# Attention output, z2 and z1 products with seven block products instead of eight, in one block of attention and gated MLP

## The chip, the cores and the metric

The kernel runs on one core of one Trainium2 chip. The metric is the device time of one execution in microseconds (us). Engines: PE is TensorE, DVE is VectorE, ACT is ScalarE, POOL is GpSimd, SP is the queue that issues most of the DMAs. PSUM is the memory into which PE writes its products, SBUF the one that holds the other tiles.

## The reference

One transformer block on 2048 tokens, model width D = 1024, bf16 in and out. Cut to what matters:

```python
h = layernorm(x) * (1 + ca) + sa
x = x + ga * (attention(h) @ wo)              # 32 heads of 128: [2048, 4096] @ [4096, 1024]
h = layernorm(x) * (1 + cb) + sb              # called h2 below
z = gelu(h @ w_in)                            # [2048, 1024] @ [1024, 3584]
z1 = z[..., :1792]
z2 = layernorm(z[..., 1792:])
g = w_sp @ z2 + b_sp[:, None]                 # [2048, 2048] @ [2048, 1792]: the "gate"
out = x + gb * ((z1 * g) @ w_out)
```

Four products come after attention: the attention output ("acc"), z2, z1, and the gate in two halves, each followed by half of the projection with `w_out`.

## The kernel before

Acc, z2 and z1 are plain products. One tile of 128 tokens is accumulated over all of the contraction in a PSUM bank, VectorE or ScalarE reads it once, and layer norm and modulation of the row follow in VectorE:

```python
# acc (L493 is the matmul), one tile of 128 tokens; cut
for n in cols:
    nc.tensor.matmul(accs[ti][n], lhs, wo_t[:, hh, sl], start=(hh == 0), stop=(hh == H - 1))
...
    nc.vector.tensor_mul(out=tmp[:], in0=accs[ti][n], in1=ga[:, sl])
    nc.vector.tensor_add(out=x1[:, sl], in0=tmp[:], in1=xts[ti][:, sl])
ln_mod(x1[:, :], mod2, hb)
nc.sync.dma_start(h2_dram[ti % 4], hb[:])          # and back with a transposing load

# z2 (L715), cut
for dc in range(KD):
    nc.tensor.matmul(zps[:], h2T[:, dc, ti * P:(ti + 1) * P], z2w[:, dc, sl],
                     start=(dc == 0), stop=(dc == KD - 1))
nc.scalar.activation(z2[:, sl], zps[:], ACT.Gelu_apprx_tanh)

# z1 (L793), cut: four banks of 512 tokens per 128 features
for dc in range(KD):
    nc.tensor.matmul(zps[:], w[:, dc, :], h2T[:, dc, q * 512:(q + 1) * 512],
                     start=(dc == 0), stop=(dc == KD - 1))
nc.scalar.activation(z1T[:, f, q * 512:(q + 1) * 512], zps[:], ACT.Gelu_apprx_tanh)
```

The gate is already computed with seven block products for eight (Winograd's form of Strassen's scheme). Operands are cut in 2 x 2 blocks; sums of blocks are formed once, seven products run, and the outputs are sums of products. The products accumulate in PSUM where they can, and VectorE saves a copy ("snap") where one partial sum serves two outputs:

```python
product(a, p, 1, True);  s = snap(p, 0)
product(c_, p, 2, True); emit(p, c_, s[:], 0, 0)               # output 11 = P1 + P2
product(a, p, 6, False); st[p]["x"] = snap(p, 0)               # P1 + P6
product(b_, p, 7, True)
product(a, p, 5, False); emit(p, b_, snap(p, 1)[:], 1, 1)      # output 22 = P1 + P6 + P5 + P7
product(a, p, 3, False); emit(p, a, b[1], 0, 1)                # output 12 = P1 + P6 + P5 + P3
product(b_, p, 4, False); emit(p, b_, x[:], 1, 0)              # output 21 = P1 + P6 + P7 + P4
```

The softmax here doesn't subtract the row's maximum and nothing guards it: scores larger than these inputs give would overflow.

## Time and profile before

| | before |
|---|---|
| time | 1838.55 us median of 4 runs (1837.13 to 1840.26) |
| PE busy | 1814.2 us, 99% of the profiled span of 1835.3 us |
| acc | 1151 to 1367 us, 0.216 us per matmul of 512 columns |
| z2 | 1367 to 1463.9 us: 512 matmuls of 448 columns, 96.9 / 512 = 0.189 us each |
| z1 | 1463.9 to 1560.6 us: 448 matmuls of 512 columns, 0.216 us each |

First the profile's page: busy time of each engine, and the busy tenths in 40 slices of the span, 45.9 us each. Acc, z2 and z1 lie in slices 26 to 34.

```profile
span 1835.3 us, 24790 instructions
...
PE 1814.2 (99%) x8926; PEld 834.8 (45%) x8926; DVE 1344.2 (73%) x2245; ACT 1135.4 (62%) x1199; POOL 32.5 (2%) x55
...
PE   7999999999999999999999999999999999999999
DVE  6998888888888988888888888544445502667664
ACT  6988999998998999999999999000003355003000
```

Read it by columns. PE is at 9 from the second slice to the last. DVE and ACT fall to 0 to 5 after attention: where the change works, only PE is full. So matmuls that are removed there should come straight off the time, as long as what replaces them fits into the other two engines.

The same by stage, from the windows of the trace (busy time of each engine inside each stretch): acc, z2, z1.

```profile
core 0: us, PE busy (x) PEld busy (x) DVE busy (x) ACT busy (x) POOL busy (x), PEclk, DMA share, GB/s
1161.00:1367.00 206.00, 206.00 (x956) 93.44 (x955) 92.73 (x166) 0.00 (x0) 8.23 (x15) 1.00 0.56 162
1367.00:1463.90 96.90, 96.90 (x514) 50.12 (x513) 59.73 (x119) 34.27 (x63) 8.77 (x16) 1.00 0.27 91
1463.90:1560.60 96.70, 96.70 (x450) 43.83 (x448) 14.82 (x24) 48.52 (x72) 0.55 (x1) 1.00 0.48 103
```

PE is busy for the whole of each stretch. The groups of instructions (last columns: busy us, mean ns of one | idle time of the engine just before them) give counts and say the same: no idle time before these matmuls.

```profile
L493 PE MATMUL acc<-wo_t,ot 128*128 128x512 bf16 x992 | 219.6, 379 | 0.0
...
L715 PE MATMUL zps<-z2w,h2T 128*128 128x448 bf16 x512 | 97.0, 352 | 0.0
L793 PE MATMUL zps<-h2T,z1w 128*128 128x512 bf16 x448 | 96.9, 379 | 0.0
```

The 379 ns is the length of one matmul's record; matmuls overlap, and what counts is the distance from one start to the next, 0.216 us for 512 columns and 0.189 us for 448.

Below, "lost" is the distance between the starts of consecutive matmuls less the pitch of the first, that is, the distance when nothing waits (columns / 2.4 + 2.6 ns, which gives the measured 0.216 and 0.189 us), summed over a stretch, without steps of one pitch where a record is missing. For the kernel before, acc, z2 and z1 lost 0.1 us, and gates and projections 5.5 us.

### The profile page before, as it was taken

Reading aid. Unit: us, or ns where it says so; the run is one execution under the profiler, and the core shown is the slowest. Engines: PE = TensorE matmul, PEld = TensorE weight load, DVE = VectorE, ACT = ScalarE, POOL = GpSimd, SP = SyncE. Lnnn points to the kernel's source line nnn. Section 1 sums busy time; section 2 is a strip of 40 time slices with the busy share of each in tenths; the row PEclk is TensorE's granted clock in tenths of the full one; section 3 lists DMA queues with packets and bytes.
Section 4 is the critical chain, followed back from the end, with each engine's and each line's share of the span. In section 5 each row is a group of like instructions: output and inputs, shape, how many; then the busy total and the mean of one; then the engine's idle time right before and its main releaser. Section 6 shows DMA issues by size and latency. Waiting matters only on the chain.

```text
span 1835.3 us, 24790 instructions
## 1 busy us (share of the span) xinstructions
PE 1814.2 (99%) x8926; PEld 834.8 (45%) x8926; DVE 1344.2 (73%) x2245; ACT 1135.4 (62%) x1199; POOL 32.5 (2%) x55
## 2 busy tenths in 40 slices
PE   7999999999999999999999999999999999999999
PEld 4444444444444444444444444444445544444444
DVE  6998888888888988888888888544445502667664
ACT  6988999998998999999999999000003355003000
POOL 1000000000000000000000000000000000000000
PEclk9999999999999999999999999999999999999999
DMA  7565465464564543555554434757423190436212
GB/s 241 139 160 127 127 162 135 135 167 121 138 163 131 163 125 93 144 164 129 149 154 135 123 108 114 225 164 204 119 64 110 73 214 1 148 94 188 75 52 75
DMA packets 431947, 245.70 MB, mean 134 GB/s; under 512 B 303440, under 2 KB 385616, under 8 KB 431824
## 3 DMA queue, kind: packets, MB, share of 16 engines
q1 hardware_dynamic: 431824, 244.13, 48.7%
q8 instruction: 69, 1.13, 0.3%
q14 instruction: 54, 0.44, 0.1%
HBM read 141.56 MB, written 52.97 MB: 106 GB/s over the span
## 4 chain that ended last, share of the span: by engine, by line
PE 93%; DMA 3%; DVE 2%; SPq 1%; issue 1%; ACT 0%; POOL 0%; DVEq 0%; POOLq 0%
PE sps L384 23%; PE ops L591 23%; PE acc L493 12%; PE qps L363 11%; PE zps L715 5%; PE bo L900 5%; PE zps L793 5%; PE a L818 4%; DMA zr<-z_dram 3%; PE b L818 2%; PE c L818 1%; DVE pacc L601 1%; DMA wm<-in_w_mod_dram 1%; PE mps L190 0%; DVE stats L143 0%
## 5 line engine op out<-in xcount | busy, mean ns | idle before, releaser
L579 ACT ACTIVATE pt<-sps 128x1024 bf16<-128x1024 f32 x1024 | 1018.9, 1024 | 105.0 <-PE sps L384 74.3
L601 DVE TENSOR_TENSOR pacc<-pacc,pt 128x1024 bf16<-128x1024 bf16 x896 | 616.4, 688 | 61.6 <-ACT pt L579 1.9
L591 PE MATMUL ops<-pt,v_sb 128*128 128x512 bf16 x2048 | 609.9, 379 | 1.2 <-DVE ou L597 1.2
L384 PE MATMUL sps<-qT,kT 128*128 128x512 bf16 x2048 | 608.9, 379 | 1.1 <-ACT pt L579 0.7
L363 PE MATMUL qps<-h1T,wq_t 128*128 128x512 bf16 x992 | 335.5, 379 | 0.5 <-DVE rec L452 0.4
L591 PEld LDWEIGHTS <-v_sb 128*128 128x128 bf16 x2048 | 200.1, 98 | 242.0 <-issue 0.3
L384 PEld LDWEIGHTS <-kT 128*128 128x128 bf16 x2048 | 199.0, 98 | 244.2 <-issue 6.7
L493 PE MATMUL acc<-wo_t,ot 128*128 128x512 bf16 x992 | 219.6, 379 | 0.0
L717 ACT ACTIVATE z<-zps 128x448 f16<-128x448 f32 x64 | 34.8, 544 | 279.3 <-PE zps L715 266.1
L363 PEld LDWEIGHTS <-wq_t 128*128 128x128 bf16 x992 | 97.0, 98 | 117.1
L493 PEld LDWEIGHTS <-ot 128*128 128x128 bf16 x992 | 97.0, 98 | 116.8
L353 DVE CAST qT<-qps 128x512 bf16<-128x512 f32 x124 | 85.7, 691 | 42.9 <-PE qps L363 42.7
L900 PE MATMUL bo<-w_out_t,z1T 128*128 128x512 bf16 (+2 forms) x476 | 97.1, 366 | 0.0
L715 PE MATMUL zps<-z2w,h2T 128*128 128x448 bf16 x512 | 97.0, 352 | 0.0
L793 PE MATMUL zps<-h2T,z1w 128*128 128x512 bf16 x448 | 96.9, 379 | 0.0
L670 DVE TENSOR_TENSOR tmp<-acc,ga 128x512 f32<-128x512 f32 x32 | 22.0, 687 | 99.4 <-PE acc L493 99.4
L749 ACT ACTIVATE w<-w 128x1024 f16<-128x1024 bf16 x32 | 32.4, 1047 | 95.3 <-DMA w<-in_B_w_sp_dram 95.3
L823 DVE SCALAR_TENSOR_TENSOR snap<-a,b_bc 128x512 f32<-128x512 f32 x42 | 28.9, 689 | 67.3 <-PE a L818 67.0
L461 DVE TENSOR_TENSOR oT<-ou,rbc 128x1024 bf16<-128x1024 f32 x62 | 75.5, 1218 | 0.4 <-DMA rbc<-rec_dram 0.4
L715 PEld LDWEIGHTS <-h2T 128*128 128x128 bf16 x512 | 50.1, 98 | 46.8
L900 PEld LDWEIGHTS <-z1T 128*128 128x128 bf16 x476 | 45.5, 98 | 51.6
L818 PEld LDWEIGHTS <-zs 128*128 128x128 f16 x448 | 43.8, 98 | 54.8 <-issue 2.1
(104 smaller groups left out, 1001.6 us busy)
## 6 DMA issues: line engine op xcount, KB each, us to landing
rbc<-rec_dram SPq DMA_DIRECT2D x64, 512.0 KB
v_sb<-in_A_v_cache_dram SPq DMA_DIRECT2D x40, 512.0 KB
oT_dram<-oT SPq DMA_DIRECT2D x62, 256.0 KB
zr<-z_dram SPq DMA_DIRECT2D x14, 1024.0 KB
sums_dram<-pacc SPq DMA_DIRECT2D x55, 256.0 KB
wm<-in_w_mod_dram SPq DMA_DIRECT2D x12, 1024.0 KB
ot<-oT_dram SPq DMA_DIRECT2D x24, 512.0 KB
wo_t<-in_A_wo_dram SPq DMA_DIRECT2D x8, 1024.0 KB
```

The lines of the kernel that those rows point to most:

```text
L353: nc.vector.tensor_copy(out=out_t[:, sl], in_=box["ps"][:])
L363: nc.tensor.matmul(box["ps"][:], wq_t[:, dc, hc:hc + DH], src[:, dc, q0:q0 + 512], start=(n == 0), stop=(n == KD - 1))
L384: nc.tensor.matmul(sps[:, j * 512:(j + 1) * 512], kts[h][:, kb * P:(kb + 1) * P], qts[(h, qh)][:, j * 512:(j + 1) * 512], start=True, stop ...
L461: nc.vector.tensor_mul(out=oT[:], in0=state[i]["ou"][:], in1=state[i]["rbc"][:])
L493: nc.tensor.matmul(accs[ti][n], lhs, wo_t[:, hh, sl], start=(hh == 0), stop=(hh == H - 1))
L579: nc.scalar.activation(pt[:], s_tiles.pop(g)[:], ACT.Exp, scale=SCALE)
L591: nc.tensor.matmul(o_ps[j][:], vs[h][:, kb, :], pt[:, j * 512:(j + 1) * 512], start=(kb == 0), stop=(kb == NKB - 1))
L601: nc.vector.tensor_add(out=pacc[:], in0=pacc[:], in1=pt[:])
L715: nc.tensor.matmul(zps[:], h2T[:, dc, ti * P:(ti + 1) * P], z2w[:, dc, sl], start=(dc == 0), stop=(dc == KD - 1))
L793: nc.tensor.matmul(zps[:], w[:, dc, :], h2T[:, dc, q * 512:(q + 1) * 512], start=(dc == 0), stop=(dc == KD - 1))
L818: nc.tensor.matmul(ps[:], zs[p][n][:, k, :], wb[n][:, k, :], start=(start and k == 0), stop=(k == 7), skip_group_check=True)
L900: nc.tensor.matmul(bo, z1T[:, f, ti * P:(ti + 1) * P], w_out_t[:, f, sl], start=(f == 0), stop=(f == NF - 1))
```

## The change

The intent: compute acc, z2 and z1 with seven block products for eight too, as the gate already does. That takes one eighth of their matmuls away. In exchange VectorE forms sums of operand blocks and adds a saved copy to three of four outputs, and ScalarE makes the copies.

The core of it, cut strongly (a new class, used by all four products):

```diff
+    class Block:
+        BANK = {1: "a", 6: "a", 5: "a", 3: "a", 2: "c", 7: "b", 4: "b"}
+        def finish(self, n):
+            ps = self.ps[self.BANK[n]]
+            if n == 1:
+                self.s = self.snap(ps, 1)
+            elif n == 2:
+                self.out(1, 1, ps, self.s)
+            elif n == 6:
+                self.x = self.snap(ps, 2)
+            elif n == 5:
+                self.out(2, 2, self.ps["b"], self.snap(ps, 3))
+            elif n == 3:
+                self.out(1, 2, ps, None)
+            elif n == 4:
+                self.out(2, 1, ps, self.x)
+            for fn in self.hooks.get(n, ()):
+                fn()
+            ...
+    def copy_snap(ps, which):                       # L801, ScalarE
+        nc.scalar.activation(t, ps, ACT.Copy)
+    def add_to(ps, snap):                           # L806, VectorE: this is what frees the bank
+        nc.vector.tensor_add(out=t, in0=ps, in1=snap)
+    ...
+    def mod_h(i, j):                                # rows 0..7: modulated after the load, on ScalarE
+        nc.scalar.activation(t[:, dc, :], t[:, dc, :], ACT.Identity, scale=..., bias=...)
+    def h_sum(c, n):                                # L982, VectorE, four per half of the tokens
+        fn(out=s[n][:], in0=a[:], in1=b[:])
+    def w2_sum(k, n):                               # L1005, VectorE, four per half of the columns
+        nc.vector.tensor_sub(out=t[n][:], in0=a[:], in1=b[:])
+    ...
+    wos[5].hooks[4] += [lambda: load_x(14), lambda: load_x(15), lambda: load_h(0)]
+    hk = wos[7].hooks                               # the last of eight acc blocks
+    hk[1] += [lambda: give_b(0, 0), lambda: mod_h(1, 0), lambda: mod_h(1, 1)]
+    hk[2] += [lambda: give_b(1, 0), lambda: load_w2(0), lambda: mod_h(0, 0)]
+    hk[6] += [lambda: give_t(2), lambda: h_sum(0, 1)]
+    hk[7] += [lambda: give_t(3), lambda: h_sum(0, 2)]
+    wos[6].hooks[4] += [lambda: w2_sum(0, 3), lambda: w2_sum(0, 1)]
+    hk[5] += [lambda: give_b(0, 1), lambda: load_w1(0, 0), lambda: load_w1(0, 1),
+              lambda: w2_sum(0, 2), lambda: h_sum(0, 3), lambda: h_sum(0, 4),
+              lambda: w2_sum(0, 4)]
+    ...
+    for n in range(8):                              # two z2 blocks to one z1 block
+        order += [z2b[2 * n], z2b[2 * n + 1], z1b[n]]
+    prev = dual(prev, order)                        # two streams of blocks, interleaved
-            nc.scalar.activation(t, t.bitcast(BF16), ACT.Identity, scale=UP)
+            nc.vector.tensor_scalar(out=t, in0=bf(t), scalar1=UP, scalar2=None, op0=ALU.mult)
```

"Hooks" are pieces of work that are emitted after a given product of a block, so they set the place of that work in each engine's order. PSUM tile "cb" holds the banks c and b of a block, and there are two such tiles: a block can start its product 2 only when the adds (L806) of an earlier block have emptied one.

Around this: rows are centred on ScalarE, z2 is normalised when it is loaded for the gate and no longer before it is stored, z2's stores move to POOL's queue, the scaling of the spatial weights w_sp moves from ScalarE to VectorE, and most tiles come out of one heap of 4 KB slots.

## The prediction

> **What bounds the kernel now.** TensorE. The page's busy shares give PE 1814.2 of 1835.3 us (99%); the chain of waits is 93% PE. The timeline and the stage windows give: attention to about 1149 us; attention-output product (acc) 1151 to 1367 us, 1001 matmuls of 512 columns at 0.216 us pitch; z2 product 1367 to 1463.9 us, 512 matmuls of 448 columns at 0.189 us; z1 product 1463.9 to 1560.6 us, 448 at 0.216 us. PE shows no idle time in acc, z2 and z1. The two gates already use seven block products instead of eight (392 matmuls each) and take 87.8 and 87.2 us against 84.7 us of pitch.
>
> **What the change does.** It gives the acc, z2 and z1 products the same seven-for-eight scheme.
> - Removed from PE: acc 1024 to 896 matmuls (128 x 0.216 = 27.6 us), z2 512 to 448 (64 x 0.189 = 12.1 us), z1 448 to 392 (56 x 0.216 = 12.1 us). Sum 51.8 us, all on the critical path: the floor is about 1787 us, if matmuls with one bf16 and one fp16 operand keep the pitch (the trace shows only equal types, both with 379 ns records).
> - Added to VectorE: operand sums (128x1024 of 2 bytes 0.69 us each; 128x2048 estimated 1.2 us), and for three of four outputs an addition of a saved PSUM copy (128x512 fp32, 0.69 us). The Trainium skill, "VectorE: DVE Perf Modes", "What auto-detection actually checks", says 16-bit two-source operations go at twice the rate; the trace agrees (1024 bf16 elements 0.688 us, 512 fp32 0.687 us).
> - Added to ScalarE: the copies out of PSUM (about 0.6 us each, by the 597 ns of the 128x512 Gelu), normalisation of z. It stays below PE. Scaling of the spatial weights moves from ScalarE to VectorE.
>
> **How much is given back.** VectorE in acc was 93 of 206 us busy; now I sum 17 to 20 us per 24.2 us block, plus 12 us of weight sums in the first two blocks and 9 us of sums for the next stage in the last. I expect 3 to 5 us of PE idle at those two ends. In z2/z1, PE needs 169.4 us and VectorE about 165 us of records, some 150 us when neighbouring independent operations overlap as in the gate's timeline (0.69 us records at 0.60 us pitch). Two z2 blocks and a z1 block cost PE 16.6 us and VectorE 12.4 us, except where the 32 pieces of spatial-weight scaling and sums (0.54 and 0.69 us) fall: there VectorE has 19 to 23 us. I expect 5 to 9 us of PE idle, mostly there. The gates stay within 2 us.
>
> Predicted: 1838.5 - 51.8 + about 11 = 1798 us, 8 in 10 between 1787 and 1813. Chances: faster by over 2% (below 1801.8) 0.63; within 2% 0.35; slower 0.02.
>
> **What would show it.** Matmul counts 128, 64 and 56 lower with unchanged mean record; acc stage 190 to 196 us; z stage 174 to 179 us; VectorE above 85% busy in the z stage, and waits of PE there for VectorE sums, clustered in the last third where the spatial weights are prepared.
>
> **What would make it wrong.** Slower mixed-type matmuls; VectorE queueing so that PE waits at every block (z stage over 185 us); late loads in acc; z2 buffers freed late, since their stores move to POOL's queue; or, the other way, VectorE's overlap hiding everything (1788 us).

## More of the kernel before

What PE waited for after attention, in the waits of PE (us in total, times, longest), is only this, in the gates:

```profile
PE a L818 <- DMA zr<-z_dram: 1.8, 6, 0.5
PE a L818 <- DVE snap L823: 1.6, 2, 0.8
```

## The result, and the profile after

| | before | after |
|---|---|---|
| time, median | 1839.22 us (13 runs, 1837.13 to 1840.80) | 1806.13 us (8 runs, 1805.33 to 1806.66) |
| ratio | | 0.9819, 95% interval 0.9810 to 0.9829 |
| PE busy | 1814.2 of 1835.3 us | 1767.0 of 1803.2 us |
| DVE busy | 1344.2 us | 1484.9 us |
| lost by PE after attention | 5.6 us | 23.9 us |

A ratio is the mean time of one kernel's fast runs over that of the other's in the same rounds, so it is not quite the ratio of the medians quoted beside it. The gain is 33.1 us, or 1.8%, just under the bound of 2% that was called "within".

```profile
span 1803.2 us, 25259 instructions
...
PE 1767.0 (98%) x8686; PEld 811.6 (45%) x8686; DVE 1484.9 (82%) x2524; ACT 1292.7 (72%) x1521; POOL 65.3 (4%) x105
...
PE   7999999999999999999999999999998999999999
DVE  6998888888888888888899888976688788667764
ACT  6888999999899999899999999511135666534700
```

After attention DVE is at 6 to 9 where it was at 4 to 5, and slice 31 of PE shows an 8. The eight is 1352 to 1397 us, just behind the end of acc. The waits of PE have a new head:

```profile
PE cb L758 <- DVE sum L806: 12.6, 12, 2.9
...
PE cb L758 <- DMA oq<-oT_dram: 1.0, 2, 0.8
```

PE waited twelve times for L806, the add of product and saved copy, because until it has run the PSUM tile "cb" is not free. By stretch (acc without its last block; the handoff from acc to z; the middle of the z stage; its last third):

```profile
1149.30:1322.00 172.70, 170.77 (x793) 76.30 (x792) 129.47 (x223) 31.97 (x45) 8.51 (x12) 1.00 0.48 139
1322.00:1373.00 51.00, 42.39 (x193) 19.09 (x192) 44.67 (x80) 26.95 (x42) 8.03 (x13) 0.97 0.66 178
...
1412.00:1466.00 54.00, 54.00 (x275) 26.68 (x273) 38.35 (x75) 36.03 (x69) 13.66 (x25) 1.00 0.59 142
1466.00:1516.00 50.00, 47.24 (x225) 21.75 (x224) 46.62 (x113) 29.29 (x55) 10.65 (x15) 1.00 0.42 122
```

The columns are those of the windows before. In the middle of the z stage, with VectorE 38.35 of 54 us busy, PE stands still for nothing. At the handoff VectorE has 44.67 of 51 us, and PE is busy for 42.39.

The account of the 33.1 us, by the measure defined above:

| | us |
|---|---|
| matmuls removed: acc 1024 to 896, z2 512 to 448, z1 448 to 392 | -51.8 |
| lost in acc up to 1322 us | +3.4 |
| lost at the handoff, 1322 to 1373 us | +11.6 |
| lost just behind it, 1373 to 1412 us | +2.7 |
| lost 1412 to 1466 us | 0.0 |
| lost where the spatial weights are prepared, 1466 to 1516 us | +3.9 |
| gates and projections: 2.5 now, 5.6 after attention before | -3.1 |
| sum | -33.3 |

The two profiled executions differ by 32.1 us (1835.3 and 1803.2 us). The account is 1.2 us over that because in the changed kernel five matmuls more (1.1 us) are still to do when these stretches begin.

Now the handoff itself, in the timeline of VectorE (start us, length us, engine, line, operation; in brackets idle time before it and what ended it). L806 is the add that frees PSUM; L1005 and L982 are one-time sums of weights and of h2.

```profile
1337.46 1.09 DVE L1005 TENSOR_TENSOR w_t<-w,w 128x1792 f16<-128x1792 bf16 x1
1338.58 1.09 DVE L1005 TENSOR_TENSOR w<-w,h_slots 128x1792 f16<-128x1792 bf16 x1
...
1340.92 0.68 DVE L806 TENSOR_TENSOR sum<-cb,snap 128x512 f32<-128x512 f32 x1
...
1342.97 1.08 DVE L1005 TENSOR_TENSOR w_t<-w,w 128x1792 f16<-128x1792 bf16 x1
...
1346.24 1.08 DVE L1005 TENSOR_TENSOR h_slots<-w,w_t 128x1792 f16<-128x1792 bf16 x1
...
1350.04 0.68 DVE L806 TENSOR_TENSOR sum<-cb,snap 128x512 f32<-128x512 f32 x1
...
1352.20 1.28 DVE L136 BATCH_NORM_STATS2 stats<-x_in 128x6 f32<-128x512 bf16 x2
...
1353.88 0.62 DVE L806 TENSOR_TENSOR sum<-cb,snap 128x448 f32<-128x448 f32 x1
```

And PE in the same stretch:

```profile
1337.76 1.68 PE L758 MATMUL a<-h_slots 128*128 128x448 bf16 x8
1341.65 3.61 PE L758 MATMUL cb<-wo_t,oq 128*128 128x512 f16 x16 [2.22 <-DVE sum L806]
...
1354.55 1.37 PE L758 MATMUL cb<-w_t,h_slots 128*128 128x448 f16 x4 [2.86 <-DVE sum L806]
1355.72 1.70 PE L758 MATMUL a<-w_t,hs 128*128 128x448 f16 x4
```

The add that PE needs at 1341.65 us is issued at 1340.92 us, behind two weight sums and two modulations of a row; the next one, at 1350.04 us, stands behind four more one-time sums and 1.31 us of waiting for ScalarE. PE's longest wait, until 1354.55 us, is for the add after that, at 1353.88 us. The operands of this add (a product and its copy) were ready by 1349.5 us, but between the two adds stand 3.1 us of work on the last rows of acc (L885, L886 and the statistics, L136). So two kinds of work stand ahead of the adds: the one-time sums and the rows. Between 1333.63 and 1363.5 us VectorE is idle for 1.31 us in all. The four matmuls at 1355.72 us take 1.70 us where four of that shape take 0.92 us elsewhere. The windows of 3.41 us show why (the figure behind POOL's is the granted clock):

```profile
1351.49:1354.90 3.41, 0.55 (x4) 0.19 (x2) 3.16 (x8) 0.06 (x1) 0.55 (x1) 1.00 0.27 101
1354.90:1358.31 3.41, 3.41 (x10) 1.32 (x9) 3.31 (x7) 2.08 (x3) 0.39 (x1) 0.50 0.23 82
```

After a window in which PE was busy for 0.55 us, the clock was half for the next one. That cost 1.7 of the 11.6 us. The Trainium skill, "TensorE: Matmul & The Clock Gate", section "What's actually happening", says that the clock is set per free-running window of 3413 ns and that half rate follows an idle window; its section "A second HAM failure mode: psum-queue depth-cycling" describes small waits for PSUM that bring the clock down. The length of the window agrees with this trace; here the window before was not idle, only 16% busy.

### The profile page after: what moved, and what is told of

It is laid out like the page before. It is cut to its first block, busy times and chain, and to the rows that moved or that the text cites. A ratio compares the mean times of both kernels' runs of the same rounds, so it can differ in the third digit from the quotient of the medians.

```text
span 1803.2 us, 25259 instructions
## 1 busy us (share of the span) xinstructions
PE 1767.0 (98%) x8686; PEld 811.6 (45%) x8686; DVE 1484.9 (82%) x2524; ACT 1292.7 (72%) x1521; POOL 65.3 (4%) x105
## 4 chain that ended last, share of the span: by engine, by line
PE 86%; DVE 9%; DMA 3%; issue 1%; SPq 1%; ACT 0%; POOL 0%; DVEq 0%; POOLq 0%; ACTq 0%
PE sps L377 23%; PE ops L649 23%; PE a L758 12%; PE qps L356 12%; PE cb L758 11%; PE bo L1343 5%; DVE pacc L660 1%; DMA oq<-oT_dram 1%; DVE sum L806 1%; DMA wm<-in_w_mod_dram 1%; DVE z_st L1096 1%; DVE stats L136 1%; DVE pacc_last L660 0%; PE mps L183 0%; DVE sum L885 0%
## 5 line engine op out<-in xcount | busy, mean ns | idle before, releaser
L637 ACT ACTIVATE pt<-sps 128x1024 bf16<-128x1024 f32 x1024 | 1018.9, 1024 | 105.9 <-PE sps L377 74.0
L801 ACT ACTIVATE snap<-a 128x512 f32<-128x512 f32 (+1 forms) x114 | 62.7, 565 | 117.2 <-PE a L758 116.1
L1202 ACT ACTIVATE zr<-zr,z_nm,z_rs 128x256 f16<-128x256 f16 x160 | 79.8, 587 | 72.0 <-DMA zr<-z_dram 58.3
L806 DVE TENSOR_TENSOR sum<-cb,snap 128x512 f32<-128x512 f32 (+1 forms) x114 | 74.3, 656 | 60.6 <-PE cb L758 36.6
L758 PEld LDWEIGHTS <-h_slots 128*128 128x128 f16 (+1 forms) x752 | 73.5, 98 | 94.3 <-issue 9.4
L1343 PE MATMUL bo<-w_out,z1T 128*128 128x512 bf16 (+2 forms) x336 | 80.4, 369 | 0.0
L758 PEld LDWEIGHTS <-zr 128*128 128x128 f16 x456 | 44.6, 98 | 55.7 <-issue 2.1
L471 DVE TENSOR_REDUCE den<-pT 128x8 f32<-128x1024 bf16 x54 | 63.9, 1183 | 0.0
L656 DVE COPY ou<-ops 128x512 f32<-128x512 f32 x63 | 43.5, 691 | 20.5 <-PE ops L649 20.4
L758 PEld LDWEIGHTS <-oq 128*128 128x128 bf16 (+1 forms) x384 | 37.1, 98 | 51.2 <-DMA oq<-oT_dram 4.6
L1276 DVE SCALAR_TENSOR_TENSOR g<-cb,snap 128x512 bf16<-128x512 f32 x42 | 29.0, 691 | 26.9 <-PE cb L758 24.7
```

Source lines behind the costliest of these rows:

```text
L471: nc.vector.tensor_reduce(out=den[:], in_=state[i]["pT"][:], op=ALU.add, axis=mybir.AxisListType.X)
L637: nc.scalar.activation(pt[:], s_tiles.pop(g)[:], ACT.Exp, scale=SCALE)
L758: nc.tensor.matmul(self.ps[self.BANK[n]], a, b, start=(n in (1, 2, 7) and k == 0), stop=(k == len(lhs) - 1), skip_group_check=True)
L806: nc.vector.tensor_add(out=t, in0=ps, in1=snap)
L1202: nc.scalar.activation(z, z, ACT.Identity, scale=z_rs[:, 8 * k + t:8 * k + t + 1], bias=z_nm[:, 8 * k + t:8 * k + t + 1])
L1343: nc.tensor.matmul(bo, z1T[ti // 8, f // 2][:, f % 2, t0:t0 + P], wout[f // 2][:, f % 2, sl], start=(f == 0), stop=(f == NF - 1))
```

## The experiments

The theories at the start. A: at the handoff VectorE has too much in-order work in front of the adds that free PSUM (eight one-time sums, row work, modulation). B: the handoff waits for the weights and rows themselves, or for the chain of the last rows, whatever else VectorE does. C: moving the scaling of the spatial weights to VectorE is what costs in the last third. Ratios below are to the kernel before in the same rounds; the changed kernel's is 0.9819 and its lost time is 11.6 us at the handoff and 3.9 us in the last third. Kernels e1 to e4 ran in one call (before: 1839.18 us), e5 to e9 in a second (1840.80), e10 and e11 in a third (1839.82), e12 (1839.01) and e13 (1840.53) alone. e12 and e13 have five timed runs each, the other experiments four. The record names a different chip for each call; the kernel before varies by 1.8 us between them, so small differences of times from different calls are read with care.

### e1: the eight one-time sums left out (wrong result)

```diff
     def h_sum(c, n):
+        if c == 0:
+            s[n] = hT[0, 1, 0]      # a loaded tile stands in
+            return
     def w2_sum(k, n):
+        if k == 0:
+            t[n] = w2[0, 0, 1]
+            return
```

> Wrong on purpose: the eight one-time operand sums that z2 and z1 need for the first half of the tokens and the first w2 half (4 of 128x2048, 4 of 128x1792, 9.2 us of VectorE records around 1328 to 1347 us) are left out and a loaded tile stands in for each. The changed kernel has 11.6 us of PE idle between 1322 and 1370 us. Theory A (VectorE's queue at the handoff: these sums stand ahead of the additions that free PSUM): 6 to 9 us less, 1797 to 1800 us, and the stretch of half clock is gone. Theory B (VectorE waits for others there, POOL's rstd and ScalarE's centring of the rows, or two wide PSUM tiles are too few): under 3 us less, 1803 us or more. Theory C (as predicted: the idle time comes with the spatial weights, late in the stage): no change.

Measured: 1799.68 us, ratio 0.9783 (0.9766 to 0.9799); relative error 0.077, as meant. The handoff lost 5.2 us, and no window there had half the clock; the last third lost 3.9 us as before. So the sums (4 x 1.08 and 4 x 1.22 = 9.2 us of VectorE time) cost 6.5 us of the kernel's time. Theory A is supported; 5.2 us at the handoff remain without them. PE in e1, at the places of its two longest waits in the changed kernel and after them:

```profile
1339.70 3.61 PE L758 MATMUL cb<-wo_t,oq 128*128 128x512 f16 x16
...
1353.55 0.92 PE L758 MATMUL cb<-w,h_slots 128*128 128x448 f16 x4 [1.81 <-DVE sum L806]
```

By the measure above, the first of the two waits falls from 2.4 to 0.1 us and the second, of 3.0 us, is gone. Two of 2.0 and 1.5 us remain (until 1353.55 and 1357.40 us); the adds for which PE waits there stand behind work on the last rows.

### e2: scaling of the first spatial weights back on ScalarE

```diff
+            if act:
+                nc.scalar.activation(t, bf(t), ACT.Identity, scale=UP)
+                return
-    z2b[12].on(1, lambda: tasks.extend(scale_w() + w_sums()))
+    z2b[12].on(1, lambda: tasks.extend(scale_w(True) + w_sums()))
```

> The 16 scalings of the first half's spatial weights go back from VectorE (0.54 us each) to ScalarE. Theory C (as predicted, 5 to 9 us lost where the spatial weights are prepared): 5 us less or more, 1801 us or below. Theory A: the 3.9 us of idle between 1465 and 1510 us shrink to 1 to 2, so 1803 to 1805 us; the handoff keeps its 11.6 us.

Measured: 1812.78 us, ratio 0.9853 (0.9838 to 0.9867): slower by 6.6 us, and both expectations missed. The last third lost 10.0 us, not 3.9. The waits of PE in 1466 to 1516 us:

```profile
PE cb L758 <- DVE sum L806: 5.6, 7, 1.8
PE a L758 <- ACT snap L801: 2.2, 2, 1.2
```

On ScalarE one piece of 128x1024 takes 1.08 us, against 0.42 us on VectorE in the changed kernel, and the copies (L801), which are what PE and the adds wait for, queue behind it. So the move to VectorE was right, and C falls.

### e3: two z1 blocks first, the w2 sums later

```diff
-    wos[6].hooks[4] += [lambda: w2_sum(0, 3), lambda: w2_sum(0, 1)]
+    wos[6].hooks[4] += [lambda: w1_sums(0, 0)]
...
+    order = [z1b[0], z1b[1]]
...
+    z1b[0].on(6, lambda: load_h(1), lambda: w2_sum(0, 3))
+    z1b[0].on(7, lambda: w2_sum(0, 1))
+    z1b[0].on(5, lambda: w2_sum(0, 2))
+    z1b[0].on(5, lambda: w2_sum(0, 4))
```

> Same arithmetic, other order: two z1 blocks go first in the z stage, since they need no w2 sums, a quarter of the statistics, and load w1 (2 tiles) rather than w2 (4 tiles) beforehand; the four w2 sums come during them. Theory A: VectorE has less to do at the handoff (4.3 us of w2 sums move, 2.9 us of w1 sums come), 3 to 6 us less, 1800 to 1803 us. Theory B: the rows' chain is the same, so within 2 us of 1806.

Measured: 1808.38 us, ratio 0.9828; the handoff lost 12.6 us, 2.8 of them by half clock. A miss, and not a clean test: three sets of w1 sums came into the place of the w2 sums, so VectorE had about as much to do there as before.

### e4: the new acc, but z2 and z1 with eight plain products

```diff
+    class Plain:
+        def run(self):
+            for q, ns in enumerate(((1, 2), (6,), (7, 4), (5, 3))):
+                ...
+                for k, (a, b) in enumerate(zip(lhs, rhs)):
+                    nc.tensor.matmul(ps, a, b, start=(k == 0), stop=(k == len(lhs) - 1))
+                self.out(i + 1, j + 1, ps, None)
-        b = Block(operands, copy_snap, out, FC)
+        b = Plain(quads, out, FC)
```

> One part of the change alone: acc keeps seven products for eight, z2 and z1 are computed with eight plain products (no sums, no PSUM copies). PE has 24.2 us more to do. If the z part of the change earns its floor less its idle time (14.8 us between 1349 and 1532 us, and some of the handoff's earlier 3.2 us), this is 1811 to 1817 us; if contention on VectorE eats all it earns, 1806 us or less.

Measured: 1818.51 us, ratio 0.9884 (0.9869 to 0.9899). The z stage lost nothing, except 6.5 us at the handoff (1.7 of them by half clock; the longest waits are 2.1 us for a Gelu on ScalarE and 1.8 us for an add of acc). So even plain products wait at the handoff, for the rows of acc: that add stands behind statistics and modulation, and the Gelu behind the centring of a row. The time is just above the 1811 to 1817 us that were expected if the z part earns what it takes off less its idle time. The z part of the change earns 1818.51 - 1806.13 = 12.4 us of the 24.2 us that it takes off PE's work.

### e8 and e9: useless adds, in the middle of acc and in its last block

Eight adds of 128x1024 (5.5 us of VectorE time), the same in both, placed in the sixth or in the eighth acc block:

```diff
+    def fill_dve():
+        nc.vector.tensor_add(out=junk[0][:], in0=mod2[:, 0, :], in1=mod2[:, 1, :])
+    for m_ in (1, 2, 6, 7):
+        wos[5].hooks[m_] += [fill_dve, fill_dve]        # e8; e9 has wos[7]
```

> Eight useless additions of 128x1024 two-byte elements (0.69 us each, 5.5 us of VectorE records) are put into the sixth of acc's eight blocks, where VectorE has some 4 us of slack per 24 us and the next block as much. Theory A (only VectorE's queue at the handoff is full): at most 1.5 us more than 1806. If VectorE is the limit all through acc, 4 to 6 us more.

> The same eight additions in acc's last block, beside the sums for z2 and z1. Theory A: 4 to 7 us more than 1806, 1810 to 1813 us, and PE idle between 1322 and 1375 us longer by about as much. Theory B (waits for POOL and ScalarE, not work): under 2 us more.

Measured: e8 1807.24 us (ratio 0.9821), e9 1808.85 us (ratio 0.9832). In the middle of acc the adds cost nothing that can be told from the spread (1805.35 to 1808.01 us). In the last block the median is 2.7 us above the changed kernel's, less than A expected; the handoff lost 13.8 us, 2.2 more, and 1.9 of these are half clock (3.6 against 1.7). The traces show why so little: in the changed kernel VectorE waits in the last block for 1.08 us (until 1330.99 us, for ScalarE's modulation) and 1.43 us (until 1333.63 us, for PE), and in e9 neither wait is there; the adds filled them. The result lies between what A and B expected. That was a hint that the order of the work matters and not only its amount.

### e5: the first weight sums on POOL

```diff
-        nc.vector.tensor_sub(out=t[n][:], in0=a[:], in1=b[:])
+        (nc.gpsimd if k in (0,) else nc.vector).tensor_sub(out=t[n][:], in0=a[:], in1=b[:])
```

> The four sums over the first half of w2 (128x1792, 1.08 us each on VectorE) run on POOL, which is 4% busy; nothing else changes. Theory A: VectorE has 4.3 us less at the handoff, 2 to 4 us less, 1802 to 1804 us, if POOL has them done by about 1355 us (estimate 3 to 4 us each, POOL's 128x1024 cast took 1.21 us); if it has not, PE waits for POOL and the time is the same or some us more.

Measured: 1814.67 us, ratio 0.9864 (0.9848 to 0.9881); the handoff lost 20.0 us. The gain that A expected did not come. POOL's timeline, one of the four sums, and then VectorE's in the same stretch:

```profile
1338.77 3.78 POOL L1005 TENSOR_TENSOR w_t<-w,w 128x1792 f16<-128x1792 bf16 x1
```

```profile
1339.03 0.68 DVE L806 TENSOR_TENSOR sum<-cb,snap 128x512 f32<-128x512 f32 x1
1339.75 3.35 DVE L885 TENSOR_TENSOR sum<-sum,ga 128x512 f32<-128x512 f32 x1
1343.13 3.95 DVE L886 TENSOR_TENSOR x_in<-sum,x_in 128x512 bf16<-128x512 f32 x1
```

POOL needs 3.8 to 4.4 us where VectorE needs 1.08, and while it works VectorE's operations with two operands in SBUF take 3.4 to 4.6 us instead of 0.7 to 1.2. The add with one operand in PSUM keeps its 0.68 us. The Trainium skill, "SBUF — State Buffer", section "SBUF: two separate sides", says that VectorE and GpSimd share one pair of ports as an exclusive lock for a whole instruction, also for a VectorE operation with two inputs in SBUF against a GpSimd operation that reads SBUF. This trace agrees: L885 ends at 1343.10 us, 0.55 us after POOL's sum does (1338.77 + 3.78 = 1342.55), and the next stretched operations end likewise just behind POOL's. So e5 slowed the very queue that it was to relieve, and it is no test of A.

### e7: the preparation of the spatial weights spread wider

```diff
-        for m in (1, 2, 6, 7, 5):
+        for m in (1, 2, 6, 7):
             b.on(m, work())
```

> The 32 pieces that prepare the spatial weights on VectorE come four to a block of z products instead of five, so over 8 blocks instead of 6.4. Theory C's remainder: the 3.9 us of PE idle between 1465 and 1510 us fall to 1 to 2.5 us, 1803.5 to 1805 us. If those waits come from something else than these pieces, no change.

Measured: 1808.93 us, ratio 0.9831. The last third lost 5.8 us, not less than 3.9: the first waits went, and one of 3.5 us came at 1507.5 us with a window of half clock, because later VectorE has the normalising, the statistics and the z1 sums to do. A miss: there was no emptier place to spread into.

### e10 and e11: half of h2 fetched and modulated one acc block earlier

```diff
-    wos[5].hooks[4] += [lambda: load_x(14), lambda: load_x(15), lambda: load_h(0)]
+    wos[5].hooks[4] += [lambda: load_x(14), lambda: load_x(15)]
+    wos[4].hooks[4] += [lambda: load_h(0)]
+    hk = wos[6].hooks                          # the modulation (mod_h) moves here from wos[7] as well
+    hk[7] += [lambda: h_sum(0, 1)]
+    hk[5] += [lambda: h_sum(0, 3)]
```

e11 in addition delays the modulation of rows 12 and 13: `after(7 if ti in (12, 13) else 2, store)`.

> Same arithmetic. The first half of h2 is fetched one acc block earlier, so that its 16 modulations on ScalarE and two of its four sums on VectorE (2.4 us of records) run in acc's seventh block instead of the eighth. Theory A, refined by the two filler runs (VectorE is over-full only from about 1336 to 1363 us): 2.4 us leave that stretch, 2 to 4 us less than 1806, 1802 to 1804 us, if it also keeps the idle below what halves the clock; less than 1 us if the waits of the rows' chain rule.

> As e10, and the modulation of two of the last four row tiles (two of 0.69 us each per tile) stands later in VectorE's queue, behind the additions that free PSUM. The work is the same, only its order differs. If order matters beside amount: 1 to 2.5 us less than e10. If VectorE is simply full until 1363 us, within 1 us of e10.

Measured: e10 1814.78 us (ratio 0.9859, 0.9843 to 0.9876), e11 1813.70 us (0.9855). The handoff did lose less (10.7 and 8.9 us), but acc before it lost 13.7 us (12.9 in e11) where it had lost 3.4. e10's queue of SP, and VectorE:

```profile
1290.32 7.42 SPq L964 DMA_TRANSPOSE h_slots<-h_dram  x2
1297.83 4.24 SPq L964 DMA_TRANSPOSE hT<-h_dram  x2
...
1302.75 0.91 SPq L836 DMA_DIRECT2D x_in<-in_A_x_dram  x2
```

```profile
1305.84 0.69 DVE L886 TENSOR_TENSOR x_in<-sum,x_in 128x512 bf16<-128x512 f32 x1 [7.32 <-DMA x_in<-in_A_x_dram]
```

Issuing the four transposing loads held the SP queue for 11.7 us, the load of the next x rows came behind them, and VectorE waited 7.3 us for it.

e11's median is 1.1 us below e10's, at the edge of what was expected if order matters, but e10's runs spread over 2.7 us and the intervals overlap, so the times decide nothing. One wait of PE does, first in e10 and then in e11:

```profile
1353.05 3.09 PE L758 MATMUL cb<-wo_t,h_slots 128*128 128x512 f16 x8 [3.09 <-DVE sum L806]
```

```profile
1350.98 1.89 PE L758 MATMUL cb<-wo_t,h_slots 128*128 128x512 f16 x8 [1.76 <-DVE sum L806]
```

In e10 two modulations of a row (0.69 us each) stand right ahead of the add that ends this wait; in e11 they come later, and the wait is 1.33 us shorter. The work is the same, only its order differs.

### e12: the same, with these loads behind the x loads

```diff
-    wos[4].hooks[4] += [lambda: load_h(0)]
+    wos[5].hooks[5] += [lambda: load_h(0)]      # after load_x(12), load_x(13)
```

> The same early fetch as e10 (first half of h2 loaded, modulated and two of its sums formed one attention-output block earlier), but its four transposing loads stand behind the x loads of the next rows on the SyncE queue, not ahead of them. Theory A (too much VectorE work between about 1336 and 1363 us): with two of the eight one-time sums (2 x 1.2 us) and ScalarE's 11 us of modulation out of that stretch, the time lost at the handoff falls from 11.6 to 7-9 us, and the attention-output stage loses no more than 5 us: 1802 to 1805 us. If the 13.7 us that e10 lost in the attention-output stage had another cause than the place of these loads in SyncE's queue, then that stage still loses over 10 us and the time stays above 1811 us. Rival (the handoff's wait is set by the last rows' own chain, not by how much else VectorE has to do): the handoff stays at 11 us or more and the time at 1806 or above.

Measured: 1806.56 us, ratio 0.9825 (0.9812 to 0.9839). Acc now lost 5.4 us (no more than 5 was expected), so the place in SP's queue was what had cost most of e10's 13.7 us. The handoff lost 10.5 us: with a quarter of the one-time sums and all of ScalarE's modulation gone from there, only 1.1 us less. By its amount of work, A expected 7 to 9; the rival, the chain of the last rows, was nearer. VectorE's timeline in e12:

```profile
1336.32 0.69 DVE L806 TENSOR_TENSOR sum<-cb,snap 128x512 f32<-128x512 f32 x1 [3.72 <-PE cb L758]
...
1340.15 1.09 DVE L1005 TENSOR_TENSOR w_t<-w,w 128x1792 f16<-128x1792 bf16 x1
1341.27 1.09 DVE L1005 TENSOR_TENSOR w<-w,w 128x1792 f16<-128x1792 bf16 x1
...
1343.61 0.68 DVE L806 TENSOR_TENSOR sum<-cb,snap 128x512 f32<-128x512 f32 x1
```

VectorE first stands idle for 3.7 us, because the next instruction in its order waits for PE, and then runs two weight sums, whose data had been there, ahead of an add that PE waits for.

### e13: e12 with the four weight sums ahead of that idle time

```diff
-    hk[7] += [lambda: give_t(3), lambda: h_sum(0, 2)]
-    wos[6].hooks[4] += [lambda: w2_sum(0, 3), lambda: w2_sum(0, 1)]
+    hk[7] += [lambda: give_t(3), lambda: h_sum(0, 2), lambda: w2_sum(0, 3), lambda: w2_sum(0, 1),
+              lambda: w2_sum(0, 2), lambda: w2_sum(0, 4)]
     hk[5] += [lambda: give_b(0, 1), lambda: load_w1(0, 0), lambda: load_w1(0, 1),
-              lambda: w2_sum(0, 2), lambda: h_sum(0, 4),
-              lambda: w2_sum(0, 4)]
+              lambda: h_sum(0, 4)]
```

> e12 with one thing moved: the four one-time sums of the second half's first weights (w2_sum, 1.08 us each) are emitted before VectorE's add for the last but one block's fourth product, where e12's trace shows VectorE idle for 3.72 us (1332.6 to 1336.3 us), and not after it; their data are loaded by then and their slots were given back two products earlier. Nothing is taken away. Theory A (the wait at the handoff is made by in-order VectorE work standing ahead of the adds that free PSUM): the two late adds of e12 (issued 1343.6 and 1351.6 us) come 2 to 4 us earlier, the loss from 1322 to 1373 us falls from 10.45 to 6 to 8 us, and the time is 1802 to 1804.5 us, below the changed kernel's 1806.1. Rival (the last rows' own chain of add, statistics, centring on ScalarE and modulation sets the wait, and the sums only fill time that would be waited anyway): the loss stays at 10 us or more and the time at 1806 or above.

Measured: 1804.56 us (1803.57 to 1804.84), ratio 0.9804 (0.9791 to 0.9818). The handoff lost 6.9 us, 3.6 less than in e12 with not one instruction fewer. VectorE in e13:

```profile
1336.48 1.09 DVE L1005 TENSOR_TENSOR w_t<-w,w_t 128x1792 f16<-128x1792 bf16 x1
1337.49 0.68 DVE L806 TENSOR_TENSOR sum<-cb,snap 128x512 f32<-128x512 f32 x1
...
1342.62 0.68 DVE L806 TENSOR_TENSOR sum<-cb,snap 128x512 f32<-128x512 f32 x1
```

The idle time is gone, and the two late adds of e12 come 1.0 us (1342.62 for 1343.61) and 3.0 us earlier (1348.60 for 1351.60), where 2 to 4 us were expected for both. The time was at the edge of what A expected (1802 to 1804.5 us). This is the fastest kernel with right results here, but by little: its median is 1.6 us below the changed kernel's, and the two intervals against before (0.9791 to 0.9818 and 0.9810 to 0.9829) overlap. The intervals of e12 and e13 overlap as well. That e13's handoff is shorter than e12's, its trace shows; that e13 beats the changed kernel is likely and not proved.

## Why the prediction was right or wrong

The median of 1806.1 us lies inside the range of 1787 to 1813 us and 8 us above the 1798 us; the gain of 1.8% fell into "within 2%", which had been given less than "faster". That the time came so near owes something to luck: 3.1 us came back in the gates, which the prediction had not counted on.

- **The bound and the floor were right.** PE bounded the kernel, matmul counts fell by 128, 64 and 56, the pitch stayed at 0.216 and 0.189 us, and fp16 with bf16 operands cost nothing extra (records of 379 and 352 ns as before). 51.8 us came off PE's work.
- **The step that failed is the size of what is given back: "about 11".** It measured 18.3 us: 23.9 us lost after attention, less the 5.6 us of before.
- **Within it, "3 to 5 us of PE idle at those two ends" of acc was the term that was too small.** Its beginning and middle cost 3.4 us (1.2 us of them at the start, about 2.2 us waiting for loads of attention's output, which were not in the sum); the end cost 11.6 us, with 2.7 us right behind it. The prediction set 9 us of sums against the 24.2 us of a whole block. The trace shows that they do not share a block evenly: VectorE stood idle for 2.5 us shortly before 1333.6 us (1.08 and 1.43 us) and then worked through to 1363.5 us with 1.3 us of pause, and every add that frees PSUM stood somewhere in that order. Without the eight sums the loss falls to 5.2 us (e1). The same kind of work in the middle of acc costs nothing that can be told from the spread (e8). Put ahead of VectorE's idle time, the same weight sums cost less (e13, 6.9 us against 10.5 in e12). Two modulations moved behind an add shorten PE's wait for it by 1.33 us (e11 against e10). So it is shown that the one-time sums cause more than half of the 11.6 us (6.4 us, e1, the 1.7 us of half clock included), and that work costs PE time by standing ahead of an add in VectorE's order. What the amount of work costs apart from its order is not isolated: e1 changed both at once, and where mainly the amount was changed, the loss moved by only 1.1 us (e12) and 2.2 us (e9). What remains in e1 and e4 (5.2 and 6.5 us), with hardly any sums, I put down to the rows of acc themselves (add, statistics, centring, modulation): the traces show this work right ahead of the adds and of the Gelu that PE waits for, but no run took that work away, so this part is read from the traces only. Nor did any run have a third "cb" tile, with which PE would depend less on each add; that two are too few (named under B in the expectation of e1) stays untested.
- **A half-rate clock after a wait was not foreseen.** It cost 1.7 us.
- **"5 to 9 us of PE idle, mostly there" for the z stage was right in mechanism and wrong in weight.** The place named, the preparation of the spatial weights, lost 3.9 us; the middle lost nothing, as expected. Together with the 2.7 us behind the handoff, during the second h2 and w2 sums, that is 6.6 us. VectorE was 83% busy (150.1 of 181 us from 1351 us), slightly below the 85% named, and the waits were for VectorE's sums, as said.
- **Gates: "within 2 us" was a little off, to the good side.** They lost 3.1 us less than before. The waits for the load of zr are gone from the waits of PE; the change loads it in halves. No run isolated this.
- **Stage times.** Acc took about 199 us (1150.6 to about 1349 us; predicted 190 to 196) and the z stage about 183 us (predicted 174 to 179), though at the handoff the two overlap.

Of the list of what would make it wrong, slower mixed types and waits at every block did not happen; late loads in acc did, at 2.2 us.

## What to carry to other kernels

When matmuls are exchanged for work on other engines, do not compare averages per stage. Look for the place where one stage ends and the next begins: there the last rows of one, the one-time preparation of the other and the operations that free PSUM meet in one in-order queue. Place one-time work ahead of an instruction on which the engine would wait anyway, and not ahead of one that frees a buffer; and look at what stands behind a long DMA issue on the same queue before moving it.

## What the Trainium skill lacked or had wrong

- "TensorE: Matmul & The Clock Gate", "What's actually happening": half rate is said to follow an idle window of about 3.4 us. Here it followed windows in which PE was busy for 0.55 of 3.41 us (changed kernel), 0.92 of 3.42 (e13) and 1.15 of 3.41 (e12); it did not follow one with 1.59 of 3.41 us. So a window need not be idle. Of all windows at full clock around the handoff in these traces, the busiest that half rate followed had 1.39 us (e9) and the least busy that it did not follow had 1.48 us (e10). The page has no such figure.
- The same page, "Back-to-back issue gap": it gives about 131 ns per matmul as the sustained spacing for 512 columns with weight loads between, and says that the isolated formula (columns / 2.4 + 2.5 ns) counts too much there. In long streams with a weight load for every matmul these traces show 0.216 us for 512 columns (448 matmuls in 96.7 us) and 0.189 us for 448 (512 in 96.9 us): the formula holds, the 131 ns do not.
- "GPSIMD Engine Reference", "Engine selection": about twice slower than VectorE for elementwise work with two inputs. For 16-bit operands of 128x1792 it was 3.8 to 4.4 us (with VectorE at work beside it) against 1.08 us, 3.5 to 4.1 times. Its figure of 2.6 cycles per element at 1.2 GHz gives an estimate of 3.9 us (1792 x 2.6 / 1.2), which agrees; the page's measured ratio, 1.96, is for 32-bit data.
- No page gives, for this chip, the time in us that a transposing load of 512x512 elements of 2 bytes holds the queue that issues it: four of them took 11.7 us of SP's queue (e10) and 11.3 us in the changed kernel, and loads behind them came that much later.
